# Retention beside the first MoE: one visit per unit instead of two interleaved ones, its outputs in the product banks' rotation, and a third input buffer

## The chip, the cores and the metric

The kernel runs on one core of a Trainium2 chip. The time is the device time of one launch in microseconds (us), taken as the median of repeated runs. Inputs are random; all arithmetic is FP32, or FP32 made of pairs of reduced-precision parts (below).

## The reference

Three layers follow one another: a retention (linear attention with a decay per head) over 8 batches of 8 heads, then a three-way max MLP, then a gated MLP.

```python
ret = scale * (q @ k.T) * D[h]            # D = gamma[h] ** (i - j) where i >= j, else 0
x = (ret @ v) as (8 * 576 tokens, 512)
h = max(max(x @ w1, x @ w2), x @ w3)      # 512 -> 768, the "first MoE"
x = h @ w_out                             # 768 -> 512
h = x @ w_in                              # 512 -> 2048
out = (h * clip(h + 3, 0, 6) / 6) @ w_out2
```

## The kernel before

**Tiles.** Retention works on 32 *units*: one batch with one pair of heads (HP = 4 pairs, so units 4t to 4t+3 belong to batch t). The 576 positions of a unit are 9 chunks of 64. A unit's q, k, v lie in one tile `raw` of 128 x 2304 FP32 (1.18 MB, loaded by two DMAs). A unit takes three kinds of matmul, all in plain FP32, which the trace records as two instructions per matmul: *scores* (2 matmuls a chunk, 64x64 tiles of the array), *outer* (2 a chunk for the first 8 chunks, 64x64 tiles, key times value) and *values* (2 a chunk, 128x64 tiles). In all 18 + 16 + 18 = 52 matmuls, 104 instructions. Between them VectorE multiplies scores by the decay mask (`masked`), runs the decay recurrence over the outer products (`states`, 16 small instructions) and scales the output (`decayed`); ScalarE and VectorE then split the output into a high and a low part in the batch's x tile (`finish`), ScalarE having scaled the keys beforehand (`decay`).

**The first MoE** works on batches of 512 tokens (t = 0 to 8; the ninth holds the last 64 tokens of each batch). A batch takes 24 *blocks* of 12 matmuls of 128x512 each: for each of six f, three *up* blocks (L492, `up`) whose outputs are maximised, and one *down* block (L508). Up block j = 0 is read out of PSUM by ScalarE (L501), j = 1 and 2 by VectorE (L503). Each product is three matmuls of split parts (L486 to L488).

**PSUM.** Of eight banks, two are a rotation for the up products (`ps_mm`, tag "mm", two buffers), four hold the down products, and two (`banks`) belong to retention. An up block takes the next bank of the rotation, and must wait until that bank's last contents were read.

**Order.** The program is written out in order by hand; every engine runs its instructions in that order. Units 0 to 7 (batches 0 and 1) are computed before the first MoE, by other code. Batches 0 and 1 of the first MoE run under a written-out plan (L618), and from t = 2 on a loop runs the 24 blocks of batch t (L709). Beside batch t the retention of batch t+1 is done: `steps(b)` (L455) makes nine steps for the four units of a batch. The step `begin` of a unit issues scores and outer of its chunks 0 to 3 and the values of the preceding unit's chunks 4 to 8; the step after it issues scores and outer of chunks 4 to 7, the scores of chunk 8 and the values of chunks 0 to 3. So there are nine stretches of retention matmuls a batch (here called *visits*), each between two MoE blocks: the first of a batch with 16 matmuls, seven with 26, the last with 10. Everything goes through the two banks `self.ps[0]` and `self.ps[1]`. The loop spreads the nine steps over the 24 blocks (L715); batch 2's nine are issued one after each block near the plan's end (L638). `load_raw` loads the next unit's input into one of two `raw` buffers, in `begin`.

**Other work in the loop.** After every third block `background()` converts one FP64 weight tile for the second MoE: four to eight VectorE instructions, ScalarE casts, GpSimd multiplies and DMAs on SyncE's queue, which issues nearly all DMAs. Low parts (`late`) are issued at the next block (`flush`).

Of the kernel before, what the change touches and what calls it, by code (L numbers as in the profile page):

```python
# [7 lines left out]
F32 = mybir.dt.float32  # L8
# [8 lines left out]
P = 128  # L17
B, H, S, D = 8, 8, 576, 64
DM, FF1, FF2 = 512, 768, 2048
NT = B * S  # L20
C = 64
NC = S // C
HP = H // 2
# [10 lines left out]
Z0, Z1, VS1, VS0, RAW = 0, S, 2 * S, 3 * S, 4 * S  # L34
# [3 lines left out]
def retention_moe_moe2(ctx: ExitStack, tc, raw, w_a, w_b, factors, masks, out):  # L38
# [3 lines left out]
    def f32(ap):  # L42
        return ap.bitcast(F32)
# [23 lines left out]
    at = tc.alloc_tile_pool(name="at", bufs=1, side="right")  # L67
    ps_mm = ctx.enter_context(tc.tile_pool(name="ps_mm", bufs=2, space=PSUM))
# [3 lines left out]
    def x_tile():  # L72
        return x_pool.tile([P, 2, KM, TB], F32R, tag="x", name="x")
# [153 lines left out]
    units = [(b, hp) for b in range(B) for hp in range(HP)]  # L227
    halves = (slice(0, D), slice(D, P))

    def load_raw(i, room=None):  # L230
        if i >= len(units) or i in raws:
            return
        b, hp = units[i]
        t = room if room is not None else at.tile([P, RAW], F32, tag="raw", bufs=2, name="raw")
        raws[i] = t

        def part(c0, c1):
            nc.sync.dma_start(out=t[:, c0:c1], in_=raw[b, hp, :, c0:c1])

        if i:  # L240
            part(VS1, RAW)
            part(Z0, VS1)
            return
        part(VS1, VS0)
        part(VS0, RAW)
        part(Z0, VS1)
# [4 lines left out]
    def decay(i):  # L251
        if i < len(units):
            k = raws[i][:, VS1:VS0]
            nc.scalar.mul(k, k, kdec_sb[:, units[i][1], NC:])

    xs = {}
    banks = [ps_at.tile([P, 512], F32, name=f"at{n}") for n in range(2)]

    class Unit:
# [24 lines left out]
                nc.tensor.matmul(ps[other, c0:c0 + C], lhsT=self.part(e, c + 1, VS1, VS0)[own, :],  # L284
                                 rhs=self.part(e, c, VS0, VS1)[own, :], start=True, stop=True)

        def keys(self, n):
            for c in range(4 * n, 4 * n + 4):
                self.scores(c, self.ps[0], c * C)
                self.outer(c, self.ps[1], c * C)  # L290

        def masked(self, c, n, ps, p0):
            t = raws[self.i]
            for e in range(2):
                own, other = halves[e], halves[1 - e]
                c0 = (Z0, Z1)[e] + c * C
                nc.vector.tensor_tensor(
                    out=t[own, c0:c0 + n * C].rearrange("p (c s) -> p c s", s=C),
                    in0=ps[other, p0:p0 + n * C].rearrange("p (c s) -> p c s", s=C),
                    in1=mask_sb[other, self.hp, None, :].to_broadcast([D, n, C]), op=ALU.mult)  # L300
# [23 lines left out]
                in0=ps[:, p0:p0 + n * C].rearrange("p (c s) -> p c s", s=C),  # L324
                in1=qdec_sb[:, self.hp, None, :].to_broadcast([P, n, C]), op=ALU.mult)


        def first_mm(self):
            self.keys(0)

        def first_rest(self):
            self.masked(0, 4, self.ps[0], 0)
            self.states(0)

        def second_mm(self):
            self.keys(1)
            self.scores(NC - 1, self.ps[0], 0)
            self.values(range(4), self.ps[1])

        def second_rest(self):  # L340
            self.masked(4, 4, self.ps[0], 4 * C)
            self.states(1)
            self.masked(NC - 1, 1, self.ps[0], 0)
            self.y = at.tile([P, S], F32, tag="yr", bufs=2, name="yr")
            self.decayed(0, 4, self.ps[1])

        def third_mm(self):
            self.values(range(4, NC - 1), self.ps[0], 4 * C)
            self.values([NC - 1], self.ps[1], 4 * C)

        def third_rest(self):
            self.decayed(4, 4, self.ps[0], 4 * C)
            self.decayed(NC - 1, 1, self.ps[1], 4 * C)
            self.finish()

        def finish(self, eng=None):
            b, hp, y = self.b, self.hp, self.y
# [13 lines left out]
    class Summed(Unit):  # L371
# [3 lines left out]
        def prepare(self):  # L375
            h = (NC - 1) // 2
            for c in [*range(h, NC), *range(h)]:
                k = self.part(1, c, None, VS1)
                nc.scalar.mul(k, k, kdec_sb[:, self.hp, c:c + 1])
# [72 lines left out]
                in1=qdec_sb[:, self.hp], op0=ALU.mult, op1=ALU.mult)  # L452
            self.finish(eng)

    def steps(b):  # L455

        us = [Unit(b * HP + hp, banks) for hp in range(HP)]
        res = []
        for hp in range(HP + 1):
            u, last = (us[hp] if hp < HP else None), (us[hp - 1] if hp else None)  # L460

            def begin(u=u, last=last):
                if u:
                    u.first_mm()
                if last:
                    last.third_mm()
                if u:
                    u.first_rest()
                if last:
                    last.third_rest()  # L470
                load_raw(b * HP + hp_of(u, last) + 1)

            res.append(begin)
            if u:
                res.append(lambda u=u: (u.second_mm(), u.second_rest(), decay(u.i + 1) if u.hp < HP - 1 else None))
        return res

    def hp_of(u, last):
        return u.hp if u else HP


    def product(ps, w, cols, terms, first, last, read=False):

# [41 lines left out]
    def blocks(t):  # L525

        res = []
        for f in range(F1):
            res += [lambda f=f, j=j: up(t, f, j) for j in range(3)]
            if f or t:  # L530
                res.append((lambda f=f: down(t, f - 1)) if f else (lambda: down(t - 1, F1 - 1)))
        return res

    with tc.manual_schedule():
# [19 lines left out]
        us = [Summed(i, pairs[i % HP if i < 2 * HP - 1 else 0]) for i in range(2 * HP)]  # L554
# [12 lines left out]
        def block(t, f, j=None):  # L567

            k = order_a.index(3 * F1 + f if j is None else 3 * f + j)
            while wa.ended < k + 1:  # L570
                wa.step()
            if j is None:
                down(t, f)
            else:
                up(t, f, j)
# [42 lines left out]
        plan = [(1, 0, j) for j in range(3)] + [(0, 0), (0, 2, 2)] + [(1, 1, j) for j in range(3)] + [(0, 1)]  # L618
# [5 lines left out]
        f = F1 - 1  # L624
        plan += [(0, f, 0), (1, f, 0), (0, f, 1), (1, f, 1), (0, f, 2), (0, f - 1), (0, f), (1, f, 2)]
        plan += [(1, g) for g in range(f)]
        decay(2 * HP)
        side = steps(2)
        start = plan.index((1, f, 0))
        for n, blk in enumerate(plan):  # L630
            block(*blk)
            if wa.ended < NA and n % 3:
                wa.step()
                if wa.ended == NA - 1:
                    wb.fetch(2)
            if blk == (0, f, 2):
                xs[2] = x_tile()
            if n >= start and blk not in ((0, f, 1), (0, f, 2)) and side:  # L638
                side.pop(0)()
        while side:  # L640
            side.pop(0)()


        def prepare(t):

            if t >= B:
                return []
            xs[t] = x_tile()
            decay(t * HP)
            return steps(t)  # L650

        def background():

# [55 lines left out]
        for t in range(2, TT):  # L709
            side = prepare(t + 1)  # L710
            todo = blocks(t)
            count, total = len(todo), len(side)
            for n, blk in enumerate(todo):
                blk()
                while side and (total - len(side)) * (count - 3) < n * total:  # L715
                    side.pop(0)()
                if t < 7 and n % 3 == 0:
                    background()
                if t == B - 1 and n in (2, 3):
                    k = slice(2 * n - 4, 2 * n - 2)  # L720
                    ends = f32(pair())
                    nc.sync.dma_start(out=ends, in_=xe_d[:, k])
                    if n == 2:
                        xs[B] = x_tile()
                    waiting.append((ends, k))
                if t == B - 1 and n in (8, 10):
                    ends, k = waiting.pop(0)
                    split(ends, xs[B][:, 0, k], xs[B][:, 1, k])
                if t == B:
                    if n == 1:  # L730
                        xv = load_x2(0, f32(x_tile()).rearrange("p a k n -> p (a k n)")[:, :KM * TS + TS])
                        load_wq(0, 0)
                    if 1 <= n <= F2:
                        load_wo()
                    if 8 <= n and n % 2 == 0 and names:
                        operand(0, xv, names.pop(0))
            while side:
                side.pop(0)()
            if t == B - 2:
                flush()  # L740
                while wb.ended < len(order_b):
                    background()
                flush()
                at.release()
                stage.release()
                ps_at.release()
                xq_pool = ctx.enter_context(tc.tile_pool(name="xq", bufs=1, side="right", reuse_waits="tile"))
                ps_x = ctx.enter_context(tc.tile_pool(name="ps_x", bufs=1, space=PSUM, reuse_waits="tile"))
                names = list(FRONT + BACK)
# [5 lines left out]
        todo = []  # L755
# [209 lines left out]
```

## Time and profile before

| | us |
|---|---|
| median of 3 runs | 1483.03 |
| runs | 1482.79, 1484.08, 1483.03 |
| the profiled execution, its own time | 1484.84 |
| its span (first to last instruction) | 1483.1 |
| outside the span in that execution | 1.74 |
| TensorE busy in the span | 1457.8 |

The profile is one execution. Times in its rows are counted from the start of the span. TensorE's matmuls are pipelined: the reported duration of one is from its start to its modelled end, and the next one starts well before that, so what a matmul costs is read from the distance between starts. In the timeline, neighbouring instructions of one line are merged into one row with a count; the row's duration is then from the first one's start to the last one's end.

### The profile page before, as it was taken

The page shows a single profiled execution, that of the slowest core. Times are in us where ns is not written, and L with a number is a line of the kernel's source. Part 1 is how long each engine was busy: PE and PEld are TensorE (multiplying, and loading weights), DVE is VectorE, ACT ScalarE, POOL GpSimd, SP SyncE. Part 2 cuts the span into 40 slices and gives each one's busy share as a digit, 9 for nine tenths or more (in the row PEclk, how much of TensorE's full clock was granted, in tenths as well). Part 3 has the DMA queues.
Part 4 walks back from the last instruction along what each step waited for, and adds up shares of the span by engine and source line. Part 5 has one row for each costly group of instructions (what it writes and reads, how often), then busy time and mean ns, then how long its engine had stood idle before and what let it go on. Part 6 is the DMA issues. An engine that isn't in the chain of part 4 may idle for free.

```text
span 1483.1 us, 24499 instructions
## 1 busy us (share of the span) xinstructions
PE 1457.8 (98%) x9680; PEld 1249.4 (84%) x9680; DVE 903.3 (61%) x1932; ACT 457.7 (31%) x881; POOL 163.8 (11%) x122
## 2 busy tenths in 40 slices
PE   7999999999999999999999999999999999999998
PEld 6678778888888888888899899899899889989997
DVE  6989668787878754223446555664664555566444
ACT  6644223434333321212222222232332223223221
POOL 3423002333332400000000000000000000000000
PEclk9999999999999999999999999999999999999999
DMA  8523235555565530136453263453436336335431
GB/s 319 181 94 114 95 114 212 200 191 213 200 215 199 189 124 18 43 121 220 148 164 114 86 235 113 135 193 114 128 100 218 116 100 228 113 108 175 115 100 43
DMA packets 94498, 219.01 MB, mean 148 GB/s; under 512 B 14128, under 2 KB 17328, under 8 KB 94384
## 3 DMA queue, kind: packets, MB, share of 16 engines
q1 hardware_dynamic: 94096, 217.10, 44.2%
q8 instruction: 77, 1.26, 0.3%
q10 hardware_dynamic: 288, 0.35, 0.1%
q14 instruction: 37, 0.30, 0.1%
HBM read 174.42 MB, written 42.99 MB: 147 GB/s over the span
## 4 chain that ended last, share of the span: by engine, by line
PE 88%; DVE 8%; ACT 2%; issue 1%; DMA 1%; POOL 0%; SPq 0%; DVEq 0%; ACTq 0%
PE mm L486 17%; PE mm L488 16%; PE mm L487 16%; PE o L806 5%; PE o L807 5%; PE o L805 5%; PE o L486 3%; PE o L487 3%; PE o L488 3%; PE p L805 3%; PE p L807 3%; PE p L806 3%; PE at L318 2%; PE at L277 2%; DVE xf L695 1%
## 5 line engine op out<-in xcount | busy, mean ns | idle before, releaser
L53 ACT CAST gp<-g 128x384 fp32r<-128x384 f32 x192 | 98.6, 513 | 337.3 <-DVE g L764 334.7
L486 PE MATMUL mm<-x,w 128*128 128x512 f32 x468 | 186.6, 399 | 0.5 <-DVE t L503 0.4
L488 PE MATMUL mm<-x,w 128*128 128x512 f32 x468 | 182.3, 390 | 0.5 <-DVE w L154 0.5
L487 PE MATMUL mm<-x,w 128*128 128x512 f32 x468 | 182.5, 390 | 0.0
L54 DVE TENSOR_TENSOR gp<-g,gp 128x384 fp32r<-128x384 f32 x192 | 107.2, 558 | 111.1 <-ACT gp L53 111.1
L771 DVE TENSOR_TENSOR cc<-mm,c 128x384 f32<-128x384 f32 x142 | 78.7, 554 | 137.8 <-PE mm L488 96.5
L806 PE MATMUL o<-w,gp 128*128 128x512 f32 x384 | 151.1, 393 | 0.0
L807 PE MATMUL o<-w,gp 128*128 128x512 f32 x384 | 150.5, 392 | 0.0
L805 PE MATMUL o<-w,gp 128*128 128x512 f32 x384 | 150.1, 391 | 0.0
L503 DVE TENSOR_TENSOR t<-mm,t 128x512 f32<-128x512 f32 x108 | 74.2, 687 | 119.0 <-PE mm L488 117.4
L486 PE MATMUL mm<-T,wq 128*128 128x384 f32 x382 | 129.4, 339 | 0.7
L776 ACT COPY c<-mm 128x384 f32<-128x384 f32 x143 | 68.5, 479 | 197.1 <-PE mm L488 197.1
L488 PE MATMUL mm<-T,wq 128*128 128x384 f32 x382 | 128.8, 337 | 0.0
L487 PE MATMUL mm<-T,wq 128*128 128x384 f32 x382 | 128.4, 336 | 0.0
L136 POOL TENSOR_TENSOR wf<-wf,wp 128x512 f32<-128x512 f32 x56 | 83.8, 1497 | 338.4 <-DVE wp L134 335.8
L486 PEld LDWEIGHTS mm<-x,w 128*128 128x128 f32 x468 | 87.8, 188 | 20.8 <-DVE t L503 1.1
L488 PEld LDWEIGHTS mm<-x,w 128*128 128x128 f32 x468 | 87.9, 188 | 19.5 <-DVE w L154 0.9
L487 PEld LDWEIGHTS mm<-x,w 128*128 128x128 f32 x468 | 87.9, 188 | 17.0
L486 PE MATMUL mm<-B,wq 128*128 128x384 f32 x286 | 96.4, 337 | 0.0
L488 PE MATMUL mm<-B,wq 128*128 128x384 f32 x286 | 96.3, 337 | 0.0
L487 PE MATMUL mm<-B,wq 128*128 128x384 f32 x286 | 96.1, 336 | 0.0
L53 ACT CAST h<-t 128x512 fp32r<-128x512 f32 x54 | 33.6, 622 | 184.1 <-DVE t L503 171.1
(170 smaller groups left out, 2960.4 us busy)
## 6 DMA issues: line engine op xcount, KB each, us to landing
wq<-wqd SPq DMA_DIRECT2D x336, 256.0 KB, 3.1
raw<-in_raw SPq DMA_DIRECT2D x55, 576.0 KB, 5.0
ws<-in_w_b SPq DMA_DIRECT2D x32, 512.0 KB, 5.5
ws<-in_w_a SPq DMA_DIRECT2D x24, 512.0 KB, 3.5
wqd<-y SPq DMA_DIRECT2D x24, 512.0 KB, 2.7
x2d<-y SPq DMA_DIRECT2D x18, 512.0 KB, 3.5
wod<-y SPq DMA_DIRECT2D x16, 512.0 KB, 2.7
w<-wod SPq DMA_DIRECT2D x16, 512.0 KB, 4.3
```

Source lines behind the costliest of these rows:

```text
L53: nc.scalar.copy(hi, full)
L54: late.append(lambda: (eng or nc.vector).tensor_tensor(out=lo, in0=full, in1=f32(hi), op=ALU.subtract))
L136: nc.gpsimd.tensor_tensor(out=frac, in0=frac, in1=f32(power), op=ALU.mult)
L486: nc.tensor.matmul(ps, lhsT=wh, rhs=xh, start=first, stop=False, skip_group_check=read)
L487: nc.tensor.matmul(ps, lhsT=wh, rhs=xl, start=False, stop=False, skip_group_check=read)
L488: nc.tensor.matmul(ps, lhsT=wl, rhs=xh, start=False, stop=last, skip_group_check=read)
L503: nc.vector.tensor_tensor(out=tmp[t, f], in0=ps, in1=tmp[t, f], op=ALU.max)
L771: nc.vector.tensor_tensor(out=c, in0=a, in1=b, op=ALU.add)
L776: nc.scalar.copy(c, ps)
L805: nc.tensor.matmul(outs[s], lhsT=gh, rhs=wo[f][:, 0, :], start=start, stop=False)
L806: nc.tensor.matmul(outs[s], lhsT=gh, rhs=wo[f][:, 1, :], start=False, stop=False)
L807: nc.tensor.matmul(outs[s], lhsT=gl, rhs=wo[f][:, 0, :], start=False, stop=stop)
```

## The change

Retention beside the first MoE no longer runs as two interleaved steps per unit. `visit(i)` issues in one stretch all values of unit i-1, then all scores and outer products of unit i. The values of chunks 0 to 7 go to a bank `full` of the product rotation, and the values of chunk 8 and the scores of unit i's chunk 8 to a second one, `small`; so a visit takes both banks of that rotation. Scores and outer products of chunks 0 to 7 take the two retention banks, 512 columns each. On VectorE, `masked` and `decayed` then work on 512 columns at once in place of twice 256; `states` keeps its 16 instructions, eight in the visit and eight in `rest(i)`, one block later. `ready(i)`, two blocks after that, scales the keys of unit i+1. In the loop the visits stand after blocks 1, 7, 13 and 19 of 24, `rest` after 2, 8, 14, 20 and `ready` after 4, 10, 16, 22. Near the plan's end the visits of units 8 to 12 stand after (1,5,0), (0,4), (1,5,2), (1,1) and (1,3); so each batch's first unit is begun beside the batch before. Visit 8 has no preceding unit, and visit 32 only has values. The tile `raw` has three buffers, and `load_raw(i + 2)` is issued at the end of visit i.

The diff, without the removed step methods of `Unit` (`keys`, `first_mm` to `third_rest`) and without the removed lines that emptied `side` at the end of each loop:

```diff
-        t = room if room is not None else at.tile([P, RAW], F32, tag="raw", bufs=2, name="raw")
+        t = room if room is not None else at.tile([P, RAW], F32, tag="raw", bufs=3, name="raw")
...
-    def steps(b):
...
+    def visit(i):
+
+        u = Unit(i, banks) if i < len(units) else None
+        last = pending.pop() if pending else None
+        small = ps_mm.tile([P, 512], F32, tag="mm", name="mm") if not last else None
+        if last:
+            full, small = (ps_mm.tile([P, 512], F32, tag="mm", name="mm") for n in range(2))
+            last.values(range(NC - 1), full)
+            last.values([NC - 1], small, C)
+        if u:
+            u.scores(NC - 1, small, 0)
+            for c in range(NC - 1):
+                u.scores(c, banks[0], c * C)
+                u.outer(c, banks[1], c * C)
+        if last:
+            last.y = at.tile([P, S], F32, tag="yr", bufs=2, name="yr")
+            last.decayed(0, NC - 1, full)
+            last.decayed(NC - 1, 1, small, C)
+            last.finish()
+        if u:
+            u.masked(NC - 1, 1, small, 0)
+            u.masked(0, NC - 1, banks[0], 0)
+            u.states(0)
+            pending.append(u)
+        load_raw(i + 2)
+
+    def rest(i):
+        if pending:
+            pending[0].states(1)
+
+    def ready(i):
+        decay(i + 1)
+
+    pending = []
...
         decay(2 * HP)
-        side = steps(2)
-        start = plan.index((1, f, 0))
+        base = 2 * HP
+        side = {(1, f, 0): [(visit, 0)], (0, f, 1): [(ready, 0)], (1, f, 1): [(rest, 0)]}
+        for n, (a, b) in enumerate(zip([(0, f - 1), (1, f, 2), (1, 1), (1, 3)], [(0, f), (1, 0), (1, 2), (1, 4)])):
+            side[a] = [(visit, n + 1)]
+            side[b] = [(rest, n + 1), (ready, n + 1)]
...
-            if n >= start and blk not in ((0, f, 1), (0, f, 2)) and side:
-                side.pop(0)()
+            for act, k in side.get(blk, ()):
+                act(base + k)
...
             xs[t] = x_tile()
-            decay(t * HP)
-            return steps(t)
+            res = {}
+            for k in range(HP):
+                for d, act in ((1, visit), (2, rest), (4, ready)):
+                    res[6 * k + d] = lambda act=act, k=k: act(t * HP + k + 1)
+            return res
...
                 blk()
-                while side and (total - len(side)) * (count - 3) < n * total:
-                    side.pop(0)()
+                if n in side:
+                    side[n]()
```

## Rows read from the trace of the kernel before

**Rows 1.** The page: its head, and busy time of each engine (share) with instruction counts.

```profile
span 1483.1 us, 24499 instructions
...
PE 1457.8 (98%) x9680; PEld 1249.4 (84%) x9680; DVE 903.3 (61%) x1932; ACT 457.7 (31%) x881; POOL 163.8 (11%) x122
```

**Rows 2.** Stretch of one batch: length, each engine's busy time (instructions), TensorE's granted clock, DMA share, GB/s.

```profile
283.00:361.00 78.00, 78.00 (x705) 63.02 (x704) 60.69 (x163) 29.43 (x53) 26.98 (x20) 1.00 0.58 204
```

**Rows 3.** Waits in 150:600: engine, line, releaser: total us, times, longest.

```profile
PE at L277 <- DVE raw L297: 0.7, 2, 0.4
```

**Rows 4.** Timeline of TensorE: start, duration, line, form, count [idle before]; a visit.

```profile
303.94 0.39 PE L486 MATMUL mm<-x,w 128*128 128x512 f32 x1
...
306.43 0.39 PE L488 MATMUL mm<-x,w 128*128 128x512 f32 x1
306.75 0.27 PE L277 MATMUL at<-raw 64*64 64x64 f32 x2
...
307.27 0.28 PE L277 MATMUL at<-raw 64*64 64x64 f32 x4
307.48 0.69 PE L318 MATMUL at<-raw 128*64 128x64 f32 x16
308.09 0.50 PE L486 MATMUL mm<-x,w 128*128 128x512 f32 x1
...
308.89 0.40 PE L486 MATMUL mm<-x,w 128*128 128x512 f32 x1
```

**Rows 5.** The same view: the last product before the first visit of two successive batches.

```profile
283.39 0.39 PE L488 MATMUL mm<-x,w 128*128 128x512 f32 x1
...
361.49 0.39 PE L488 MATMUL mm<-x,w 128*128 128x512 f32 x1
```

**Rows 6.** The same view: 16 values matmuls in one run, then 64x64 tiles.

```profile
21.25 1.15 PE L318 MATMUL o<-raw 128*64 128x64 f32 x32
22.33 0.43 PE L387 MATMUL mm<-room 64*64 64x256 f32 x2
```

**Rows 7.** The same view: first and last product around batch 2's visits, and one of them.

```profile
153.95 0.39 PE L488 MATMUL mm<-x,v 128*128 128x512 f32 x1
...
176.92 0.33 PE L277 MATMUL at<-raw 64*64 64x64 f32 x4 [0.36 <-DVE raw L297]
...
205.29 0.39 PE L488 MATMUL mm<-x,w 128*128 128x512 f32 x1
```

**Rows 8.** Timelines of TensorE and VectorE: last product of an up block, and its readout.

```profile
143.07 0.39 PE L488 MATMUL mm<-x,v 128*128 128x512 f32 x1
...
143.50 0.69 DVE L503 TENSOR_TENSOR t<-mm,t 128x512 f32<-128x512 f32 x1 [0.63 <-PE mm L488]
...
324.75 0.39 PE L488 MATMUL mm<-x,w 128*128 128x512 f32 x1
...
327.18 1.48 DVE L503 TENSOR_TENSOR t<-mm,t 128x512 f32<-128x512 f32 x2
```

**Rows 9.** Groups by line and form: count | busy us, mean ns | idle before.

```profile
L297 DVE TENSOR_TENSOR raw<-at,masks_sb 64x256 f32<-64x256 f32 x96 | 40.5, 422 | 42.2 <-PE at L277 20.3 <-PE at L318 14.6 <-PE at L284 6.3
...
L427 DVE TENSOR_TENSOR raw<-o,w 64x512 f32<-64x512 f32 x6 | 4.1, 689 | 3.1 <-issue 3.0
...
L443 DVE TENSOR_TENSOR yr<-o,w 128x512 f32<-128x512 f32 x4 | 2.7, 678 | 0.0
```

**Rows 10.** Timeline of VectorE: half of a unit's states, and a weight tile's first instructions.

```profile
308.48 1.95 DVE L311 SCALAR_TENSOR_TENSOR raw<-raw,at 64x64 f32<-64x64 f32 x8
310.45 0.46 DVE L297 TENSOR_TENSOR raw<-at,masks_sb 64x64 f32<-64x64 f32 x2
...
313.33 0.42 DVE L113 TENSOR_SCALAR wp<-ws 128x512 uint32<-128x512 uint32 x1
...
315.21 0.68 DVE L503 TENSOR_TENSOR t<-mm,t 128x512 f32<-128x512 f32 x1
```

**Rows 11.** Waits in 150:600 again, on a unit's input.

```profile
ACT raw L254 <- DMA raw<-in_raw: 15.5, 4, 4.2
```

More of the change, by code (lines that the diff above doesn't have):

```diff
@@ L285, in outer @@
                                  rhs=self.part(e, c, VS0, VS1)[own, :], start=True, stop=True)
[L287 to L290, printed above, removed]
         def masked(self, c, n, ps, p0):
@@ L325, in decayed @@
                 in1=qdec_sb[:, self.hp, None, :].to_broadcast([P, n, C]), op=ALU.mult)
[L328 to L354, printed above, removed]
         def finish(self, eng=None):
@@ L453, in last_rest @@
             self.finish(eng)
-    def steps(b):
[L457 to L479, printed above, removed]
+    def visit(i):
[28 more added lines that the diff above has]
+    pending = []
     def product(ps, w, cols, terms, first, last, read=False):
@@ L637, in retention_moe_moe2 @@
                 xs[2] = x_tile()
-            if n >= start and blk not in ((0, f, 1), (0, f, 2)) and side:
-                side.pop(0)()
-        while side:
-            side.pop(0)()
+            for act, k in side.get(blk, ()):
+                act(base + k)
         def prepare(t):
             if t >= B:
-                return []
+                return {}
             xs[t] = x_tile()
-            decay(t * HP)
-            return steps(t)
+            res = {}
[3 more added lines that the diff above has]
+            return res
         def background():
@@ L711, in retention_moe_moe2 @@
             todo = blocks(t)
-            count, total = len(todo), len(side)
             for n, blk in enumerate(todo):
                 blk()
-                while side and (total - len(side)) * (count - 3) < n * total:
-                    side.pop(0)()
+                if n in side:
+                    side[n]()
                 if t < 7 and n % 3 == 0:
@@ L736, in retention_moe_moe2 @@
                         operand(0, xv, names.pop(0))
-            while side:
-                side.pop(0)()
             if t == B - 2:
```

## The prediction

> **What bounds the kernel now.** First the page: TensorE is busy for 1457.8 of 1483.1 us [rows 1], so time can only come from work that TensorE no longer does or does more densely. Next the stretch of one batch in the loop: TensorE is busy for all 78.00 us of 78.00 at full clock (1.00, the 2.4 GHz level), VectorE for 60.69, ScalarE for 29.43 [rows 2]. The list of waits has next to nothing for TensorE in the retention: 0.7 us on VectorE's masks is the longest entry, and it is two waits near the plan's end [rows 3]. "Busy" hides overheads, however, since a matmul's modelled duration runs over the gap to the next one. So the third view is the timeline, read by the distance between starts.
>
> In a block, products start 0.226 us apart (303.94 to 306.43, eleven steps), a block of twelve taking 2.72 us [rows 4]. Two batches' first visits are 78.10 us apart [rows 5]. Twenty-four blocks are 65.2 us of that, and so the nine visits cost 12.8 to 12.9 us per batch, 1.4 each, with no engine reported as idle. One visit taken apart [rows 4], counted from 306.66, where the next product would have started: 0.09 us until the first 64x64 matmul (306.75); 0.58 for scores and outer of four chunks and the scores of chunk 8 (to the last start, 307.27 + 0.28 - 0.22 = 307.33; a small matmul's duration is 0.22); **0.15 to switch** from 64x64 to 128x64 tiles (307.48); 0.47 for the values of four chunks (last start 307.48 + 0.69 - 0.22 = 307.95); 0.14 until the next product (308.09); and 0.13 because the first products come slowly (308.89 is 2.46 after 306.43 in place of four steps, 0.91; the visit costs 1.55 in all). So a visit has a **fixed price of 0.36** (0.09 + 0.14 + 0.13) and a switch of 0.15, against about 0.9 of matmuls.
>
> **The change part by part.** *Fewer visits.* The matmuls stay the same, 52 per unit. The 54 visits of six batches become 25. What a chunk costs: 16 values matmuls (eight chunks) in one run take 1.15 - 0.22 = 0.93 us, 0.116 a chunk [rows 6]; scores plus outer of a chunk take the same, since 0.58 for four chunks and two matmuls more leaves 0.116 to 0.12 each [rows 4]. A full new visit is then: fixed 0.36; values of nine chunks 0.93 + 0.12 = 1.05; switch from 128x64 to 64x64 tiles 0.15 (after the run of rows 6 the last start is 21.25 + 0.93 = 22.18 and the next tile size starts at 22.33); keys of nine chunks 0.58 + 4 x 0.117 = 1.05. Sum 2.61, and I take 2.63 for roundings. There are 23 of them (60.5), one with keys only (visit 8: 0.36 + 1.05 = 1.41) and one with values only (visit 32: 1.41): **63.3 us**. Before, without waits: 6 x 12.8 = 76.8. Gain **13.5 us**. Bounds: the switch in the new direction could cost a visit's whole fixed price, 0.36 and not 0.15, which takes 23 x 0.21 = 4.8 off; or could be hidden, which adds 3.4. I take 0.15, the row that shows just this direction.
>
> *Waits of batch 2 that go.* From 153.95 to 205.29 there are 13 blocks (35.3 us) and nine visits [rows 7]: 51.34 - 35.3 = 16.0 for the visits, where the loop's nine cost 12.8. The 3.2 us more are waits: there a visit follows each block and needs VectorE to have finished the masks and states of the visit before it (one such wait is marked in rows 7). After the change these five visits stand two or three blocks apart. Gain up to **3.1**; VectorE becomes the term to watch. Its chain for a unit there, from the moment the values are done: scaling 0.68 + 0.21, masks 0.46 + 2 x 0.69, states 1.95, low part of x 0.69, one more readout or low part 0.69, states again 1.95 [rows 9, 10], together 8.0, and then TensorE needs another 0.8 to finish the last values that wait for those states: 8.8. TensorE's own period is 2 x 2.72 + 2.63 = 8.1. But only the values of chunks 5 to 8 need the second half of the states, and the first of them starts 0.7 into the visit, so 0 to 0.7 us each is lost at three visits. I take 0.5 in all (bounds 0 and 2.1).
>
> *The product rotation: the added wait.* A visit takes both product banks. Behind a down block both have long been read. But behind an up block (visits after blocks 1 and 13: ten, and one in the plan) `small` is the bank which that block has just filled, and TensorE cannot write it before VectorE has read it; everything later in TensorE's order is queued behind. Times from the start of the last product: the readout starts 0.43 after it and ends 1.12 after it when VectorE is free (143.07, 143.50 + 0.69) [rows 8]. The values of chunk 8 would start at 0.23 + 0.09 + 0.93 + 0.06 = 1.31. So the wait is covered by the values of eight chunks, with 0.1 to 0.2 us to spare including a signal of about 0.05. If VectorE is late that cover is gone: at the latest readout shown (324.75 to 327.18 + 0.69 = 327.87, 3.12 after) the visit waits 3.12 + 0.05 - 1.31 = 1.86 us [rows 8]. How late will it be? Between a visit after a down block and the readout before the next visit lie six blocks and a visit, 19 us, and in it VectorE has 4.7 (scaling, masks, half the states), 1.95 (the other half), 0.69 x 4 (two readouts, the low parts of x and h), one weight tile of 1.9 (313.33 to 315.21) and one of at most 3.3 with its sums: 14.6 us [rows 9, 10]. The order leaves the last of it, 1.9, free to run during the block before the readout. So VectorE is idle when the product ends. I take 0.05 for each of eleven visits, **0.5** (bounds 0 and 20).
>
> The next block needs `full` read: its values end 1.25 + 0.22 after the last product, the scaling ends at 1.51 + 0.68 = 2.2, and the block's first product starts at 2.7. Covered by the scores and outer, 0.5 to spare. `small` is used a block later still.
>
> A rule speaks against this step. The rows show the readout with 0.1 to 0.2 us to spare. The Trainium skill, "Perfetto Trace Analysis", section Matmuls, says that independent matmul groups should rotate through different PSUM banks so that the evacuation of one overlaps the next group's matmuls; a visit that takes both banks leaves the block before it no such overlap but the visit itself. By the row the cost is about nothing; by the rule it is a wait at each visit, and that is the first rival.
>
> *VectorE.* `masked`: four instructions of 256 columns (0.42 each) become two of 512 (0.69); `decayed` likewise [rows 9]. That is 0.3 + 0.15 per unit, 11 us of VectorE's time, all of it beside TensorE's work. Its share of the loop stays at 78%, 60.69 of 78.00 becoming about 59 of 75.8 [rows 2].
>
> *Third buffer and moved loads.* ScalarE waited 15.5 us in four places for a unit's input [rows 11], and TensorE never for ScalarE there. The input is now asked for a visit earlier; nothing on the path. On SyncE's queue a load now waits for the values matmuls of its own visit, at most 2.6 us, with xe stores, weight fetches and x2 stores queued behind; these have blocks of 2.72 us to spare. In the first 70 us, unit 5's input no longer waits for unit 0 and may land in front of other transfers: bounds -4.2 and +4.2 us (the longest wait on an input) [rows 11]; I take 0, since unit 5 is the sixth to be used.
>
> **Sum.** 13.5 + 3.1 - 0.5 - 0.5 = **15.6 us**. The profiled execution has a span of 1483.1 and a time of 1484.84; the span becomes 1467.5. The median of the runs, 1483.03, is 1.8 under that execution's time, and the same 15.6 from it gives **1467.4 us**, 1.05% less.
>
> **The rivals.** *The readout decides (slower).* Place: `small` behind an up block, and VectorE's order. If VectorE reaches the readout as late as it once does now, eleven visits wait 1.86 each, 20.5 us, and the sum is 16.6 - 20.5: 1487 us. It decides from a mean wait of 16.6 / 11 = 1.5 us on. For: readouts do come 2 us late now, and nobody notices, because the rotation hides them. Against: the late ones follow a weight tile with its sums or a stretch of states, which the new order puts a block or more ahead. By the section Matmuls of "Perfetto Trace Analysis" in the Trainium skill this is what should happen. 8%.
>
> *VectorE still sets batch 2's stretch, and small waits remain in the loop.* The full 2.1 there, 0.2 at every visit (4.6), or the dearer switch (4.8): gain 9 to 12, about 1472. 14%.
>
> *It does not do what it says.* The visits' cost is not TensorE's own but a wait that the profile hides, such as an engine that would be late anyway; then the path is unchanged: 1483. Against it stands that a batch's time is the sum of its blocks and visits to 0.1 us. 4%.
>
> *More.* Switch hidden, no waits at all: 1463. 6%. The forecast itself, 1465 to 1470, has 68%.
>
> **How the numbers follow.** A measurement of this kernel can tell 0.2%, 3 us, from no change. Faster: 68 + 14 + 6 = 88; same 4; slower 8. The range takes the forecast, most of the second rival and the upper half of "more": 1463 to 1474.
>
> **What would show it.** TensorE's timeline should have 25 visits of about 104 instructions, values first, with 2.6 us between what would have been the next product's start and its start; the batch period should be 75.8 us in place of 78.1; the waits should have no TensorE entry over 1 us on L503 or on `decayed`. It is wrong if a visit behind an up block shows an idle gap before its last four values instructions, if the switch from 128x64 to 64x64 tiles shows more than 0.15 us, or if the period between batch 2's visits exceeds 8.1 us.

## The result, and the profile after

The changed kernel takes 1467.77 us (median of five runs, 1467.40 to 1468.42) against 1482.79 us for the kernel before, measured beside it (1482.62 to 1484.08): a ratio of 0.9898, 95% interval 0.9884 to 0.9913. The forecast was 1467.4 us. The profiled execution after has a time of 1467.40 us and a span of 1465.6; its page begins with the span and the engines' busy time (before: [rows 1]).

```profile
span 1465.6 us, 24403 instructions
PE 1442.2 (98%) x9680; PEld 1246.2 (85%) x9680; DVE 896.4 (61%) x1860; ACT 458.1 (31%) x881; POOL 160.9 (11%) x122
```

TensorE runs the same 9680 matmul instructions in 15.6 us less busy time; its share stays at 98%. The stretch of one batch, from the last product before a batch's first visit to the same product of the next batch (length, then busy time and instructions of TensorE, its weight loads, VectorE, ScalarE and GpSimd, granted clock, DMA share, GB/s), answers to [rows 2, 5]:

```profile
275.48:351.32 75.84, 75.84 (x706) 62.79 (x704) 59.75 (x151) 29.56 (x53) 26.29 (x20) 1.00 0.62 211
```

75.84 us in place of 78.10, at the same granted clock of 1.00. One visit in TensorE's timeline (start, duration, line, form, count), to be held against [rows 4]:

```profile
275.48 0.39 PE L463 MATMUL mm<-x,w 128*128 128x512 f32 x1
275.80 1.27 PE L313 MATMUL mm<-raw 128*64 128x64 f32 x36
277.00 0.27 PE L277 MATMUL mm<-raw 64*64 64x64 f32 x2
...
278.04 0.22 PE L277 MATMUL at<-raw 64*64 64x64 f32 x2
278.19 0.50 PE L461 MATMUL mm<-x,w 128*128 128x512 f32 x1
278.53 0.40 PE L462 MATMUL mm<-x,w 128*128 128x512 f32 x1
```

The next product would have started at 275.71. Values begin 0.09 later; their last start is 275.80 + 1.27 - 0.22 = 276.85; the other tile size follows 0.15 after it (277.00); scores and outer run 1.04 to their last start; 0.15 more to the next product (278.19), and 0.11 to 0.13 lost on the slow product after it. Together 2.61 us, the same at 18 of the 23 full visits to 0.01 us. Some of the products that follow still start about 0.01 late each; counted to the end of the next block, a full visit takes 2.64, which is what the batch's length shows too (24 blocks of twelve products at 0.2266 us are 65.26 of the 75.84; a quarter of the other 10.58 is 2.64). The waits of TensorE between 150 and 600 us (engine, tile and line, releaser: total us, times, longest) are a single row, where [rows 3] had another:

```profile
PE mm L461 <- DVE yr L317: 0.7, 1, 0.7
```

Summed over TensorE's timeline, with each visit counted by how far it pushes the end of the block behind it, the visits cost 64.7 us in place of 80.1: 15.4 us less. (Counted only to the sixth product behind each visit, as all costs of a visit below are, it is 64.19 in place of 79.99.) The rest of the 17.5 us between the two spans lies elsewhere: the product ahead of visit 8 starts at 151.91 us after and at 153.95 before [rows 7], in code that differs only in `raw`'s buffers. In the profiles of the ten variants of the changed kernel below, which leave this stretch alone or change only the buffers, the moment lies anywhere between 151.47 and 153.28, and in that of the kernel before with a third buffer at 152.83, so most of the 2 us is a difference between executions; the medians differ by 15.0.

### The profile page after: what moved, and what is told of

Same layout as the page of the kernel before. It is cut to its first block, busy times and chain, and to the rows that moved or that the text cites. A ratio compares the mean times of both kernels' runs of the same rounds, so it can differ in the third digit from the quotient of the medians.

```text
span 1465.6 us, 24403 instructions
## 1 busy us (share of the span) xinstructions
PE 1442.2 (98%) x9680; PEld 1246.2 (85%) x9680; DVE 896.4 (61%) x1860; ACT 458.1 (31%) x881; POOL 160.9 (11%) x122
## 4 chain that ended last, share of the span: by engine, by line
PE 46%; DVE 4%; ACT 1%; issue 0%; ACTq 0%
PE mm L461 7%; PE mm L463 7%; PE mm L462 7%; PE o L782 5%; PE o L783 5%; PE o L781 5%; PE p L781 3%; PE p L783 3%; PE p L782 3%; DVE xf L674 1%; DVE T L54 1%; DVE g L740 1%; DVE g L739 0%; DVE cc L747 0%; DVE gp L54 0%; ACT gp L53 0%
## 5 line engine op out<-in xcount | busy, mean ns | idle before, releaser
L478 DVE TENSOR_TENSOR t<-mm,t 128x512 f32<-128x512 f32 x108 | 74.1, 686 | 138.3 <-PE mm L463 138.3
```

Source lines behind the costliest of these rows:

```text
L478: nc.vector.tensor_tensor(out=tmp[t, f], in0=ps, in1=tmp[t, f], op=ALU.max)
```

## The experiments

The theory: a stretch of retention costs a fixed price and a switch beside its matmuls, and having fewer of them is the whole gain; the rotation costs nothing as long as VectorE reads the product bank in time. The rivals: the gain comes from waits or from the buffers, or the rotation and VectorE already take part of it back. Each kernel was measured beside the kernel before; a comparison between kernels of different sets goes by the two ratios. The edits are against the changed kernel where nothing else is said.

**Two stretches per unit again (e1_split_keys).**

```diff
-    def visit(i):
+    def visit(i, n=NC - 1):
...
-            for c in range(NC - 1):
+            for c in range(n):
...
-            u.masked(0, NC - 1, banks[0], 0)
-            u.states(0)
...
+    def more(i, n=4):
...
+            for c in range(n, NC - 1):
+                u.scores(c, banks[0], c * C)
+                u.outer(c, banks[1], c * C)
+            u.masked(0, NC - 1, banks[0], 0)
+            u.states(0)
...
-                for d, act in ((1, visit), (2, rest), (4, ready)):
+                for d, act in ((1, lambda i: visit(i, 4)), (2, more), (3, rest), (4, ready)):
```

The second stretch stands one block behind the first, and `rest` another block behind it.

> The changed kernel, but in the loop (units 13 to 31) each visit does only chunks 0 to 3 of the keys' matmuls, and a second stretch after the next block does chunks 4 to 7. No matmul is added; VectorE's masks and states move one block later. Theory A (a stretch of retention matmuls has a fixed price of 0.36 to 0.37 us, whatever is in it): 19 more stretches, 19 x 0.37 = 7.0 us, 1474.8 us; TensorE's timeline shows 0.32 to the first small matmul and a slow first product in each of them, and no new wait. Theory B (the gain came from the waits of batch 2 and from VectorE's larger instructions, the number of stretches is no matter): 1467.8 us.

Measured: 1493.38 us, ratio 1.0064 (1.0049 to 1.0079), far above both expectations. The trace takes it apart. A second stretch costs 0.849 us each time and a first one 2.16 to 2.19 where it doesn't wait for `small`, mostly 2.16 to 2.17, together 3.01 in place of 2.61: **0.40 more per extra stretch**, 7.6 us for 19. That is the fixed price as theory A has it, 0.37, with 0.02 to 0.04 of wait on `full`. The other 16.4 us of the visits' 24.0 are new waits, at eight visits behind up blocks alone (the row counts TensorE's idle time; one of the visits lost 1.3 us more behind its wait, below):

```profile
PE mm L313 <- DVE t L488: 13.5, 8, 1.9
```

Here the product rotation does decide: `small` waits for the readout (L488 in this kernel, L478 in the changed one). Why the readout is late stands with the last experiments. Outside the visits, eight blocks start 0.14 to 0.17 us late, 1.3 us in all, where ScalarE reads a product bank late.

**Keys ahead of the values (e2_keys_first).** The same instructions; values are issued last, those of chunk 8 first among them.

> The changed kernel with the order inside a visit turned round: scores and outer products first, then the values of chunk 8, then those of chunks 0 to 7 into the bank called full. The same matmuls, the same banks. Theory A (the readout of the full bank is late unless the scores and outer products stand between it and the next product): every one of the 23 full visits now ends as visit 32 does, which has no scores and shows 0.90 us in place of 0.15 before the next product: 23 x 0.75 = 17 us more, about 1485 us. The wait for small behind an up block, on the other hand, has 1.2 us more cover. Theory B (the order within a visit is no matter, the rotation has slack): 1467.8 us.

Measured: 1490.84 us, ratio 1.0049. Full visits in the loop cost 3.48 to 3.58 in place of 2.61. The values end, and the next product needs `full` (timeline of TensorE, a visit's end):

```profile
207.13 1.27 PE L313 MATMUL mm<-raw 128*64 128x64 f32 x36
209.20 0.50 PE L462 MATMUL mm<-x,w 128*128 128x512 f32 x1 [0.79 <-DVE yr L317]
```

The last value starts at 208.18 and the product 1.02 later, where the changed kernel takes 0.15. So in the changed kernel the 1.04 us of scores and outer behind the values are what covers the scaling of `full`. The 19 full visits of the loop explain 17 of the 22.5 us by which the visits are longer; three visits near the plan's end, inside which TensorE idles 1.5 to 2.1 us, are 1.5 to 2.2 dearer and make up the rest.

**The readout made longer (e3_reread1, e4_reread3).** In the ten loop visits behind an up block, VectorE's readout is issued twice; in e4, with a factor of 3 in the same line, four times.

```diff
-        nc.vector.tensor_tensor(out=tmp[t, f], in0=ps, in1=tmp[t, f], op=ALU.max)
+        for _ in range(1 + 1 * again[0]):
+            nc.vector.tensor_tensor(out=tmp[t, f], in0=ps, in1=tmp[t, f], op=ALU.max)
```

> The changed kernel, but at blocks 1 and 13 of each batch in the loop, before a visit behind an up block, VectorE does the maximum over the product bank twice (the second time changes nothing), so that this bank comes free some 0.61 us later; ten places. Theory A (the readout ends 1.12 to 1.19 us after the last product's start, and the values of chunk 8 would start at 1.30): the visit waits 1.19 + 0.61 + 0.05 - 1.30 = 0.5 us, ten times, 5 us in all, 1472.8 us, and the wait stands before the last four values instructions. Theory B (there is more cover than that, TensorE does not wait): 1467.8 us, VectorE's extra 6 us being hidden.

> As the one before, with the maximum done four times at those ten places, so that the bank comes free 1.83 us later, about as late as the latest readout in the kernel before (1.9 us late). Theory A: each visit waits 1.7 us, 17 us in all, 1485 us: the whole gain of the change is gone, which is the point from which the readout would decide. Theory B (TensorE has other work or cover): well under 1475 us.

Measured: 1474.81 us (ratio 0.9941) and 1497.57 (1.0101). One re-read costs 0.715 us at each of the ten visits, its whole duration: **there is no margin left**. In e3, one such readout on VectorE, and the last product ahead of it on TensorE (timelines):

```profile
277.97 1.41 DVE L480 TENSOR_TENSOR t<-mm,t 128x512 f32<-128x512 f32 x2
277.46 0.39 PE L463 MATMUL mm<-x,w 128*128 128x512 f32 x1
```

It ends at 279.38, 1.92 after the last product's start, and the visit loses 0.72: the readout must end 1.20 after that start, for the visit to lose nothing. In the changed kernel it ends at 1.19 to 1.21 at these ten visits. The mechanism of the first rival is there, and it is linear. In e4 it is worse than linear: five of the ten visits lose 2.17, five lose 3.6 to 3.7. The stretches of one of the dear visits and of a cheap one (columns as in the batch stretch above):

```profile
280.50:284.20 3.70, 1.79 (x36) 1.26 (x34) 3.60 (x7) 0.37 (x1) 2.50 (x2) 1.00 0.93 306
284.30:286.40 2.10, 2.10 (x72) 1.94 (x72) 1.15 (x4) 0.62 (x1) 0.00 (x0) 0.61 0.80 264
286.40:287.80 1.40, 1.40 (x5) 1.16 (x4) 1.25 (x2) 0.00 (x0) 0.00 (x0) 0.50 0.90 283
...
244.20:246.20 2.00, 2.00 (x75) 1.77 (x76) 1.63 (x5) 0.62 (x1) 0.00 (x0) 1.00 0.80 264
```

After an idle of 1.95 us the granted clock, the last number but two, is 0.61 and then 0.50, which is the lower level of 1.2 GHz; after an equal idle at 244 us it stays at 1.00. The price of a late readout thus has a second part of about 1.5 us that falls on some waits and not on others. The expectation had neither this nor the missing margin, and was 12.6 us short.

By the Trainium skill, "Perfetto Trace Analysis", section Matmuls, independent matmul groups should rotate through different PSUM banks so that one's evacuation overlaps the next one's matmuls. The runs with a later readout agree: e3 loses 0.715 us a visit and e4 2.17 or more. Where it ends by 1.21 us, in the changed kernel, taking both banks costs the full visits of the loop 0.00 to 0.014 each.

**The third buffer (e5_before_buf3, e6_after_buf2).** The third `raw` buffer alone in the kernel before; and the changed kernel with two buffers, the load issued for the next unit and not the one after.

> The kernel before with the third input buffer alone. Theory A (no input is waited for on TensorE's path; the 2 us by which the changed kernel's profiled execution is ahead before its first visit come from how fast the very first loads land, which differs from run to run): within 1 us of the kernel before, 1482.8 us. Theory B (the third buffer lets unit 5's input be asked for 8 us earlier and that pulls the first 45 us forward): 2 us less, 1480.8 us.

> The changed kernel with two input buffers, and each input asked for one visit later (unit i+1 at the end of visit i), as two buffers allow. Theory A (the third buffer is not what pays): the loop's visits stay at 2.61 us each, as an input lands 5 to 6 us after it is asked for and is scaled three blocks later; at batch 2's visits, two blocks apart, ScalarE may wait for it and TensorE with it, at most 1 us at each of three: 1467.8 to 1471 us. Theory B (the visits need the third buffer): waits at each visit, over 1475 us.

Measured: 1484.32 us, ratio 1.0004 (0.9995 to 1.0013), and 1468.31, ratio 0.9897 (0.9883 to 0.9910). The buffer alone does nothing, and without it the gain is whole; two visits of e6 take 0.15 to 0.16 longer. Two buffers with the load for unit i + 2 weren't tried.

**VectorE's instructions in halves (e7_halves).** `masked` and `decayed` on 256 columns at a time, as before the change; TensorE's order is untouched.

```diff
-            last.decayed(0, NC - 1, full)
+            last.decayed(0, 4, full)
+            last.decayed(4, 4, full, 4 * C)
...
-            u.masked(0, NC - 1, banks[0], 0)
+            u.masked(0, 4, banks[0], 0)
+            u.masked(4, 4, banks[0], 4 * C)
```

> The changed kernel with VectorE's masks and scaling of 512 columns cut again into twice 256, as in the kernel before: three instructions more per unit, 11 us of VectorE's time in all. Theory A (all of that is beside TensorE's work): within 1 us of 1467.8 us, at most 1 us more from batch 2's visits and visit 32. Theory B (VectorE's time is what the change gained): 1475 us or more.

Measured: 1471.98 us, ratio 0.9920 against 0.9898. Seven visits behind up blocks lose 0.39 to 0.43 each, the two waiting visits near the plan's end 0.65 and 0.53 (in the changed kernel 0.23 and 0.20), the last one 0.87 (0.74). So in this order of instructions the shorter VectorE time is needed; e10 below has another order. VectorE's timeline ahead of such a visit, in the changed kernel and then in this one, shows why; the last products start at 313.40 and 315.96:

```profile
303.83 0.41 DVE L201 TENSOR_TENSOR s<-wf 128x256 f32<-128x256 f32 x1
...
309.15 1.52 DVE L113 TENSOR_SCALAR wp<-ws 128x512 uint32<-128x512 uint32 x1
311.85 0.95 DVE L114 TENSOR_SCALAR wf<-ws 128x512 uint32<-128x512 uint32 x1 [1.18 <-POOL y L154]
312.72 0.68 DVE L132 SCALAR_TENSOR_TENSOR wf<-ws,wf 128x512 f32<-128x512 uint32 x1
313.33 0.68 DVE L134 SCALAR_TENSOR_TENSOR wp<-ws,wp 128x512 uint32<-128x512 uint32 x1
313.93 0.68 DVE L478 TENSOR_TENSOR t<-mm,t 128x512 f32<-128x512 f32 x1
```

```profile
306.78 0.41 DVE L201 TENSOR_TENSOR s<-wf 128x256 f32<-128x256 f32 x1
...
314.80 0.95 DVE L114 TENSOR_SCALAR wf<-ws 128x512 uint32<-128x512 uint32 x1 [1.19 <-POOL y L154]
...
316.87 0.68 DVE L480 TENSOR_TENSOR t<-mm,t 128x512 f32<-128x512 f32 x1
```

The weight tile that is converted behind the block before stands right in front of the readout. Its second instruction waits for GpSimd's products of the tile before (`y`, L154), and those follow VectorE's sums (L201), which follow the states and the masks. From the sums to that instruction it is 8.02 us in both kernels (303.83 to 311.85, 306.78 to 314.80). The sums start 9.57 us ahead of the last product in the changed kernel and 9.18 in this one, and the readout slides by the same 0.39: its end moves from 1.21 to 1.59 after the last product, and the visit loses 1.59 - 1.20 = 0.39.

The Trainium skill, "Perfetto Trace Analysis", section Optimizing Scalar/DVE Operations, says that where VectorE isn't saturated but causes bubbles elsewhere, breaking up instructions may let work end sooner. VectorE is at 60 of 76 us here, and breaking them up made bubbles of 0.39 to 0.43 us at seven visits: here the measurement goes the other way. With the conversion elsewhere (e10) these seven are gone.

**The last visit's values in retention's own banks (e8_last_own).**

```diff
-            full, small = (ps_mm.tile([P, 512], F32, tag="mm", name="mm") for n in range(2))
+            full, small = (ps_mm.tile([P, 512], F32, tag="mm", name="mm") for n in range(2)) if u else banks
```

> The changed kernel with one line more: visit 32, which has only values, puts them into the two retention banks, which are free then, and not into the product rotation. Theory A (its 0.75 us of waiting comes from the next product needing the bank that the visit has just filled): the visit costs 1.41 us in place of 2.16, the time is 0.7 us less, 1467.1 us, which only the timeline can tell. Theory B (the wait has another cause, such as ScalarE's or the x tile's): no change in the gap before the next product.

Measured: 1467.65 us, ratio 0.9892: not told apart by the time. In the trace the one wait of the list is gone. The last visit in the changed kernel and in this one:

```profile
560.18 1.27 PE L313 MATMUL mm<-raw 128*64 128x64 f32 x36
562.12 0.50 PE L461 MATMUL mm<-x,v 128*128 128x512 f32 x1 [0.68 <-DVE yr L317]
```

```profile
561.20 1.27 PE L313 MATMUL at<-raw 128*64 128x64 f32 x36
562.40 0.50 PE L461 MATMUL mm<-x,v 128*128 128x512 f32 x1
```

From the first value to the next product it takes 1.20 in place of 1.94: 0.74 us saved.

**The weight tile moved out of the readout's way (e9_split_moved, e10_halves_moved, e11_own_moved).** One line, in e1's, e7's and e8's kernel:

```diff
-                if t < 7 and n % 3 == 0:
+                if t < 7 and n % 3 == 2:
                     background()
```

> The keys of chunks 4 to 7 in a second stretch one block later (as in e1_split_keys, 1493.4 us), and the weight tile converted after blocks 2, 5, 8, ... instead of 0, 3, 6, ... of a batch, so that its VectorE instructions no longer stand directly ahead of the readout of block 13. Theory A (the readout of an up block came 2 us late only because the conversion, held by GpSimd, stood in front of it): the waits at visits behind up blocks go, and what stays is the price of 19 extra stretches of about 0.4 us, 7.5 us over the changed kernel, 1475 us. Theory B (VectorE is late there because of the masks and states that were moved a block later, whatever stands between): the visits behind up blocks still wait and the time stays at 1485 to 1493 us.

> VectorE's masks and scaling in halves of 256 columns (as in e7_halves, 1472.0 us), with the weight tile converted after blocks 2, 5, 8, ... of a batch. Theory A (the longer instructions cost time only because they push the conversion, and behind it the readout, past the moment at which the second bank is needed): the seven waits of 0.4 us in the loop go (2.8 us), those of the plan's two visits and of the last visit stay, about 0.9 us over the changed kernel: 1468.7 us. Theory B (the wait depends on VectorE's total work): 1472 us as before.

> The changed kernel with the last visit's values in the retention banks and the weight tile converted after blocks 2, 5, 8, .... The visits behind up blocks get a margin of 2 us, which no wait uses: by theory A the full visits stay at 2.61 us and the time is that of e8_last_own, 1467 to 1468 us. If the order of the conversion costs TensorE something by itself (a late low part, a late weight tile), it is above 1469 us.

Measured: 1475.66 us (ratio 0.9945, against e1's 1.0064), 1469.74 (0.9908, against e7's 0.9920) and 1467.03 (0.9889, 0.9874 to 0.9904). Theory A holds in e9 to 0.7 us: the 16.4 us of waits on `small` are gone, and the 19 extra stretches remain at 0.40. VectorE ahead of a visit, in e1 and then in e9, with last products at 282.05 and 278.09:

```profile
274.57 0.41 DVE L201 TENSOR_TENSOR s<-wf 128x256 f32<-128x256 f32 x1
...
282.59 0.94 DVE L114 TENSOR_SCALAR wf<-ws 128x512 uint32<-128x512 uint32 x1 [1.18 <-POOL y L154]
...
284.66 0.68 DVE L488 TENSOR_TENSOR t<-mm,t 128x512 f32<-128x512 f32 x1
```

```profile
274.46 0.42 DVE L201 TENSOR_TENSOR s<-wf 128x256 f32<-128x256 f32 x1
...
277.20 0.68 DVE L134 SCALAR_TENSOR_TENSOR wp<-ws,wp 128x512 uint32<-128x512 uint32 x1
278.58 0.69 DVE L488 TENSOR_TENSOR t<-mm,t 128x512 f32<-128x512 f32 x1 [0.70 <-PE mm L473]
```

In e1 the sums start 7.48 us ahead of the last product (masks and states were moved a block later), 8.02 later the conversion goes on, and the readout ends 284.66 + 0.68 - 282.05 = 3.29 after the last product: 3.29 - 1.20 = 2.09, the wait that the visits show (2.06 to 2.07). In e9 nothing stands between, and VectorE waits for TensorE (0.70) and not the other way round. Eight visits behind up blocks still lose 0.08 to 0.13, now at the first value and not at the last four: ScalarE, with the conversion's casts now ahead of its copy, reads the bank that becomes `full` late (ScalarE, then TensorE):

```profile
277.87 0.56 ACT L486 COPY t<-mm 128x512 f32<-128x512 f32 x1
278.49 0.69 PE L313 MATMUL mm<-raw 128*64 128x64 f32 x16
```

The copy ends at 278.43, and the first value starts 0.40 after the last product in place of 0.32. In e10 all 19 full visits of the loop are at 2.615 again. Its last 1.0 us over the expectation lies on ScalarE too. In four batches ScalarE reads a bank late, and the block that needs it starts 0.20 to 0.24 us late and loses 0.11 more on a slow first product, 1.3 us in all. In this one ScalarE's copy ends at 290.71, and the product would have started at 290.56 (ScalarE, then TensorE):

```profile
290.09 0.62 ACT L478 COPY t<-mm 128x512 f32<-128x512 f32 x1
290.33 0.39 PE L465 MATMUL mm<-x,w 128*128 128x512 f32 x1
290.76 0.50 PE L463 MATMUL mm<-x,w 128*128 128x512 f32 x1
```

In e11, which has the conversion in the same place but VectorE's instructions whole, no block starts late in this way. TensorE's list of waits between 150 and 600 us is empty there (waits of 0.2 us, which two visits near the plan's end keep, are too short for it and are read from the distances); its time can't be told from that of the changed kernel, 0.9889 against 0.9898.

## Why the prediction was right, and where it was not

**Fewer visits.** Right in every term. The visit was put at 2.63 us and takes 2.64, counted to the end of the next block; the switch in the new direction takes the 0.15 that one row had shown, and neither bound was reached. e1 and e9 show the fixed price by itself. Before and after the visits' sums are 80.1 and 64.7 us; the prediction's were 76.8 + 3.1 and 63.3 + 1.0.

**Waits of batch 2.** Right within its bounds: of the three visits in question two wait, 0.23 and 0.20, together 0.43 for the 0.5 taken. The named reason, values waiting for the unit's states, holds at one of them, the visit behind a down block whose last product starts at 180.58 (VectorE's states, then TensorE's values):

```profile
180.01 1.97 DVE L306 SCALAR_TENSOR_TENSOR raw<-raw,at 64x64 f32<-64x64 f32 x8
180.90 1.47 PE L313 MATMUL mm<-raw 128*64 128x64 f32 x36
```

The states end at 181.98, the last two values start at 182.03 and later, and the values take 1.47 us instead of 1.27. At the other, behind an up block, the reason was one that the prediction didn't name here: the readout queued behind the states on VectorE (timeline of VectorE, last product at 172.29):

```profile
171.15 1.97 DVE L306 SCALAR_TENSOR_TENSOR raw<-raw,at 64x64 f32<-64x64 f32 x8
173.04 0.68 DVE L478 TENSOR_TENSOR t<-mm,t 128x512 f32<-128x512 f32 x1
```

It ends 1.43 after the last product, 0.23 past 1.20. The periods of these visits, 8.29 and 8.26 us, are over the 8.1 that was named as a sign of error.

**The product rotation.** The price was right (0.05 per visit taken, 0.00 to 0.014 measured in the loop), its reasons were wrong, and that it came out is in part luck. The margin was put at 0.1 to 0.2 us past a readout that ends at 1.12, and that readout was taken from a place with no visit behind it [rows 8]. At the loop's ten visits behind up blocks it ends at 1.19 to 1.21, and no earlier where VectorE had been idle for 6.12 us (TensorE's last product, VectorE's readout):

```profile
540.90 0.39 PE L463 MATMUL mm<-x,w 128*128 128x512 f32 x1
541.39 0.69 DVE L478 TENSOR_TENSOR t<-mm,t 128x512 f32<-128x512 f32 x1 [6.12 <-PE mm L463]
```

(1.19 is from the unrounded times; these rounded rows give 1.18.) So the margin to 1.20 is 0.01. And "VectorE is idle when the product ends" does not hold: the step counted VectorE's work in the 19 us, 14.6, and took the remainder to lie where it was wanted. At seven of the ten visits VectorE still converts a weight tile when the product ends, at six of them held up 1.18 to 1.19 us by GpSimd. It comes free just in time: the readout ends 0.02 late, at 1.21, at three of them and on time at the others. A sum of busy times could not show this; the chain of sums, GpSimd's products and conversion could, from rows of the same view. How little was left e7 shows: 0.39 us more ahead of the readout made waits at seven visits.

**Values-only visit.** "The next block needs `full`: covered by the scores and outer" holds for the 23 full visits. Visit 32 has none behind its values and waits 0.74 us: the prediction listed this visit at 1.41 and gave it the cover that it lacks.

**VectorE.** Its share came out as forecast (59.75 of 75.84, forecast about 59 of 75.8), but "all of it beside TensorE's work" is wrong. Without the wider `masked` and `decayed`, e7 is 0.22% slower than the changed kernel by the two ratios, 3.3 us, and its visits cost 67.85 us in place of 64.19 (counted to the sixth product).

**Third buffer.** Nothing, as taken; e5 and e6 bear it out.

**The rivals.** "The readout decides" didn't come to pass, but it was nearer than 8% says: moving the masks and states by one block (e1) called it up at once and took back more than the whole gain. Its price per wait was also too low where the granted clock falls to 0.50 behind the wait. "Does not do what it says" and "the dearer switch" are excluded by the visit's rows.

The errors that remain are small and cancel in part: waits of 1.21 us in the visits (0.43 + 0.74 + 0.04) where 1.0 was taken, full visits 0.01 dearer than put, and visits of the kernel before at 80.1 us where 79.9 was read. Of the forecast's 15.6 us the trace's visits show 15.4 and the medians 15.0; that difference is within what two profiles differ by ahead of the first visit.

## What to carry to other kernels

Where a saturated TensorE interleaves small matmuls of other tile sizes, count the stretches: each detour has a price of its own, here 0.36 us and 0.15 more for a second tile size, which no idle time shows and which is read from distances between starts. When such a detour borrows the banks of a rotation, write down the moment by which the last readout must end (here 1.20 us after the last product) and follow, instruction by instruction and across engines, what stands ahead of that readout; an engine at 79% can still be the one that is late. Put work that waits for a third engine behind the readout, not in front of it.

## What the runs showed of the hardware that was not expected

The switch from 128x64 to 64x64 tiles costs the same 0.15 us as the reverse, and the return to full 128x128 products 0.15 and a slow product. A stretch of 32 small instructions costs 0.849 us between two products at whichever block it stands. After idles of 1.8 to 2.0 us TensorE's granted clock fell to 0.50 in five of ten visits in e4 and in one of seven in e1, and stayed at 1.00 in the others with equal idles; what tells them apart stays open. The idles of 0.5 us in e3 left the clock alone in all ten, and so did three idles of 1.5 to 2.1 us at e2's visits near the plan's end.

With VectorE idle, the readout of an up block starts 0.49 to 0.50 us after the last product's start ahead of the loop's visits, and 0.43 after it in the row that the prediction used; what makes the difference stays open.
